# A gated layer's first product in block form: eleven block products for twelve, seven of them over two feature tiles

## The chip, the cores and the metric

The kernel runs on one core of a Trainium2 chip (trn2). The metric is the time of one execution on the device in microseconds (us). A core has a matrix engine (TensorE, PE in the profile, with its weight loads as PEld), VectorE (DVE), ScalarE (ACT) and GpSimd (POOL); SyncE (SP) issues most transfers. PE reads SBUF and writes PSUM, and each engine runs its own program in a fixed order, waiting on semaphores.

## The reference

Two stages. The first is a delta-rule recurrence over 768 steps for 4 x 8 heads of 48 features. The second is a gated two-layer network over its 3072 token rows.

```python
k_n = k / (np.linalg.norm(k, axis=-1, keepdims=True) + 1e-06)
for t in range(S):                       # S = 768, D = 48, batch 4, heads 8
    y[:, :, t] = np.einsum('bhd,bhde->bhe', q[:, :, t], state)
    v_old = np.einsum('bhde,bhd->bhe', state, kt)
    state = state + bt[:, :, :, None] * np.einsum('bhd,bhe->bhde', kt, vt - v_old)
x = y.transpose(0, 2, 1, 3).reshape(3072, 384)
h = x @ w_in                             # 384 x 2048
g = h * np.cos(h)
return g @ w_out                         # 2048 x 384
```

The inputs moe_w_in and moe_w_out arrive as 64-bit floats, which the kernel reads as pairs of 32-bit words and narrows on the chip.

## The kernel before

**Recurrence.** The steps are cut into 24 units of 32 steps (C), and two units make a pair: 12 pairs of 256 token rows (TOK). For each unit small matmuls form the Gram blocks (`gram`), pass the keys and queries through the state (`through_state`), solve (`solve`), update the state (`update`) and form the output (`within`). For each pair a triangular inverse is formed on POOL (`invert`, with the tiles `part` and `z`), between two trips through DRAM: g out and gb back, z out and zt back. `features` turns a unit's output into the layout that the network needs, the tile x_ffn (`xts[p]`): 128 features x 3 feature tiles (KT) x 256 rows.

**First gated layer** (`hidden`). The 2048 hidden features are 16 tiles of 128 (FT). For pairs 1 to 11 the layer takes two tiles at a time into one PSUM bank: for each, three matmuls of 128x128 weights over all 256 rows, accumulated over the feature tiles. Pair 0 alone takes four tiles for one unit, so 128 rows (`hidden_one`). Two banks (tag h) alternate. Each bank is then gated in four steps: `hidden_turns` (ACT, PSUM to whole turns), `hidden_rest` (DVE, the rest of the turn), `hidden_cos` (ACT, two instructions), `hidden_gate` (DVE, times h, into the tile g_ffn). The bank is held until the last step. All h are scaled by SCALE = 256, from the way the weights are narrowed.

**Second layer.** For pair 0 it is plain (`output`). For pairs 1 to 11 it is done in seven block products for eight (`product`), over units 1 and 2, even and odd hidden tiles, and two halves of the output columns: `left_sum` (DVE) forms sums of gated blocks in place, `right_sum` sums of the weights once, and `collect` adds the products up. `left(p, k, a)` picks a block from the gate tile.

**The order.** The program of every engine is written out by `Order`, a planner: each task has an engine, a cost, dependencies, buffers that it makes and uses, and a due time; it plays the tasks in simulated time and emits them in the order in which they start. `BASE`, `START`, `FIRST` and `STEP` set the due times of the gated work, `W_IN`, `W_OUT` and `LOADS` those of the weights, `bufs` the count of buffers of each tag. `STICK` lets PE stay among small or large matmuls a little longer, and `count` and `stall` model how PE's instructions are fetched in blocks of 256. `gated(p)` adds the tasks of a pair's first layer, `strassen(p)` those of its second.

**Buffers.** Gate tiles, weights on their way (`pairs`) and squares for the norms (`ksq`) share the tag g, with GATES = 9 slots of 128 x 1024. Keys wait in four tiles `kps`, each for a pair.

Of the kernel before, what the change touches and what calls it, by code (L numbers as in the profile page):

```python
# [46 lines left out]
class Order:  # L47
# [13 lines left out]
    STICK = 2.885  # L61
# [26 lines left out]
    def count(self, key):  # L88
        if key == ("state", 0):
            return 0  # L90
        return self.COUNT[key[0]] * (2 if key[:2] == ("hidden", 0) else 1)
# [139 lines left out]
def kernel(  # L231
# [45 lines left out]
    GATES = 9  # L277
# [35 lines left out]
    kps = [const.tile([128, 2, H, DP], FP, name=f"kp{i}") for i in range(4)]  # L313
# [87 lines left out]
    w_sum = const.tile([128, FT // 2, 3, HM], FP, name="w_sum")  # L401
    p_out = psum.tile([128, 2, 256], FP, name="p_out", tag="o", bufs=1)
# [196 lines left out]
    def invert(m, tag, columns):  # L599

        a, z = gbs[m], zs[m]
        eng = nc.gpsimd if tag is None else nc.vector
        for j in columns:
            rows = j // SPLIT + 1
            shape = [128, rows, C - 1 - j]
            if tag is None:
                part = work.tile([128, ROWS * C // 2], FP, name="part")  # L610
            else:
                part = ffn_pool.tile([128, ROWS * C // 2], FP, name="part_v", tag="o")
            part = part[:, 0 : shape[1] * shape[2]].rearrange(
                "p (r i) -> p r i", i=shape[2]
            )
            eng.tensor_tensor(  # L616
                out=part,
                in0=z[:, 0:rows, j, None].to_broadcast(shape),
                in1=a[:, j, None, j + 1 :].to_broadcast(shape),
                op=ALU.mult,  # L620
            )
            behind = z[:, 0:rows, j + 1 :]
            eng.tensor_tensor(out=behind, in0=behind, in1=part, op=ALU.subtract)  # L623
# [145 lines left out]
    def step_of(tile, p):  # L769
        return tile.rearrange("p a (b t) -> p (a b) t", t=128) if p == 0 else tile  # L770

    def hidden(p, f):
        if p == 0:
            return hidden_one(f)
        p_h = p_hs[p, f] = bank("h", [128, 2, TOK], "p_h")
        for i in range(2):
            for t in range(KT):
                nc.tensor.matmul(  # L778
                    p_h[:, i],
                    w_in[:, t, (f + i) * 128 : (f + i + 1) * 128],  # L780
                    xts[p][:, t],
                    start=(t == 0),
                    stop=(t == KT - 1),
                )


    TURN = 1.0 / (2.0 * math.pi * SCALE)

    def hidden_turns(p, f):
        turns[p, f] = step_of(ffn_pool.tile([128, 2, TOK], I32, name="turns"), p)  # L790
        nc.scalar.activation(turns[p, f], p_hs[p, f], AF.Copy, scale=TURN)  # L791

    def hidden_rest(p, f):
        r = rests[p, f] = step_of(ffn_pool.tile([128, 2, TOK], FP, name="r"), p)
        nc.vector.scalar_tensor_tensor(  # L795
            out=r, in0=p_hs[p, f], scalar=TURN, in1=turns.pop((p, f)),
            op0=ALU.mult, op1=ALU.subtract,
        )
# [6 lines left out]
    def hidden_gate(p, f):  # L805
        k = f // 2 % 4 if p == 0 else f // 4
        if (p, k) not in gates:
            gates[p, k] = ffn_pool.tile(
                [128, 4, TOK], FP, name="g_ffn", tag="g", bufs=GATES
            )  # L810
        if p == 0:
            out = gates[p, k][:, :, f // 8 * 128 : (f // 8 + 1) * 128]
        else:
            out = gates[p, k][:, f % 4 : f % 4 + 2]
        nc.vector.tensor_tensor(  # L815
            out=out,
            in0=rests.pop((p, f)),
            in1=p_hs.pop((p, f)),
            op=ALU.mult,
        )  # L820

# [25 lines left out]
    def left(p, k, a):  # L847

        unit, odd_tile = a // 10 - 1, a % 10 - 1
        return gates[p, k][:, odd_tile::2, unit * 128 : (unit + 1) * 128]  # L850
# [28 lines left out]
    def product(p, x, part):  # L879
        a, b = PRODUCTS[x]  # L880
        p_o = product_out(p, x)
        for e in range(4 * part, 4 * part + 4):
            nc.tensor.matmul(  # L883
                p_o,
                left(p, e // 2, a)[:, e % 2],
                right(e, b),
                start=(e == 0),
                stop=(e == FT // 2 - 1),
                skip_group_check=True,
            )  # L890

    def left_sum(p, x, k):
        to, one, two, op = {
            1: (21, 21, 22, ALU.add),
            2: (11, 21, 11, ALU.subtract),
            3: (22, 22, 11, ALU.subtract),
            4: (12, 12, 11, ALU.subtract),
        }[x]
        nc.vector.tensor_tensor(  # L899
            out=left(p, k, to), in0=left(p, k, one), in1=left(p, k, two), op=op  # L900
        )
# [40 lines left out]
    def store(p, i, cols=slice(0, DM)):  # L942
# [11 lines left out]
            x=2, turns=2, r=2, g=GATES, o=2, o_out=2,  # L954
# [5 lines left out]
    W_IN, W_OUT, LOADS = 68.978, 54.441, -24.919  # L960
    PLAIN = range(1)
    outs_done = [None]
    START = 60.385
    FIRST, STEP = 2.515, 5.309
# [127 lines left out]

    def gated(p):
        for f in range(0, FT, 2):
            deps = [("features_out", 2 * p + 1)]
            new = f % 4 == 0
            if p == 0:
                deps = [("features_out", f // 8)]
                deps += [("add", t) for t in range(KT * (f // 2 % 4 + 1))]
                new = f < 8  # L1100
            if p or f:
                deps.append(("hidden", p if f else p - 1, f - 2 if f else FT - 2))
            key = (p, f)
            add(("hidden", *key), "PE", 2.62, lambda f=f: hidden(p, f), deps,
                makes=[("h", ("h", *key))], uses=[("x", p)],
                due=BASE[p] + f // 2 * (STEP if p else FIRST))
            add(("turns", *key), "ACT", 0.65, lambda f=f: hidden_turns(p, f),
                [("hidden", *key)], makes=[("turns", ("turns", *key))])
            add(("rest", *key), "DVE", 0.73, lambda f=f: hidden_rest(p, f),
                [("turns", *key)], makes=[("r", ("r", *key))], uses=[("turns", *key)])  # L1110
            add(("cos", *key), "ACT", 1.45, lambda f=f: hidden_cos(p, f), [("rest", *key)])
            add(("gate", *key), "DVE", 0.73, lambda f=f: hidden_gate(p, f),
                [("cos", *key)] + ([] if new else [("gate", p, f - 2 if p else f - 8)]),
                makes=[("g", ("gates", p, f // 4 if p else f // 2))] if new else [],
                uses=[("h", *key), ("r", *key)], due=BASE[p] + f // 2 * STEP + 8)
        if p in PLAIN:
            plain(p)
        else:
            strassen(p)
# [27 lines left out]
    def strassen(p):  # L1147
# [4 lines left out]
        for step, x in enumerate(products(p)):  # L1152
            tag = "h" if p == LAST and (p + step) % 2 else "o"
            for part in range(2):
                ks = (2 * part, 2 * part + 1)
                deps = [last] if last else []
                if x in (1, 2, 4):
                    deps += [("gate", p, 4 * k + f) for k in ks for f in (0, 2)]
                else:
                    deps += [("left", p, {6: 2, 5: 1, 3: 4, 7: 3}[x], k) for k in ks]  # L1160
                for e in (4 * part, 4 * part + 2):
                    if x in (1, 2, 3):
                        deps += [("add", 12 + t) for t in range(2 * e + 4)]
                    deps.append(("right", {6: 2, 4: 4, 5: 1, 7: 3}.get(x, 1), e))
                last = ("out", p, step, part)
                add(last, "PE", 1.31, lambda x=x, part=part: product(p, x, part), deps,
                    makes=[] if part else [(tag, ("p_o", p, x))],
                    uses=[("gates", p, k) for k in ks],
                    due=due(step + 0.5 * part))
                for k in ks:  # L1170
                    if x == 1:
                        add(("left", p, 1, k), "DVE", 0.46, lambda k=k: left_sum(p, 1, k),
                            [("gate", p, 4 * k), ("gate", p, 4 * k + 2)])
                        add(("left", p, 2, k), "DVE", 0.46, lambda k=k: left_sum(p, 2, k),
                            [("left", p, 1, k), last])
                    elif x in (2, 4):
                        sx = {2: 4, 4: 3}[x]
                        add(("left", p, sx, k), "DVE", 0.46,
                            lambda k=k, sx=sx: left_sum(p, sx, k), [("left", p, 2, k), last])
# [28 lines left out]

    def weights(t):
# [16 lines left out]
    for p in sorted(PLAIN):  # L1226
        gated(p)
    weight_sums()
    for p in range(len(PLAIN), NU // 2):
        gated(p)  # L1230
# [63 lines left out]
```

## Time and profile before

| what | before |
|---|---|
| runs shown, us | 699.57, 694.07, 699.24; median 699.24 |
| profiled execution, us | 697.96 |
| its span, us, and mean granted PE clock | 696.1, 0.99 |
| PE busy | 627.9 us, 90% |
| PE weight loads busy | 554.6 us, 80% |
| DVE busy | 418.1 us, 60% |
| ACT busy | 266.3 us, 38% |
| POOL busy | 341.4 us, 49% |
| bytes moved | 52.41 MB, mean 75 GB/s |

The page of the profile shows one execution. Its lines with forty digits cut the span in slices of 17.4 us, each digit the busy share in tenths. A group's line gives source line, engine, operation, tile written <- tiles read, shapes and count, then after the bar the busy time and the mean length of one instruction in ns, and after the second bar the engine's idle time before them with what ended it. A matmul of float32 appears as two instructions, each with its own weight load. Instructions of PE are pipelined, so that a matmul's length is more than its spacing to the next one.

### The profile page before, as it was taken

The page shows a single profiled execution, that of the slowest core. Times are in us where ns is not written, and L with a number is a line of the kernel's source. Part 1 is how long each engine was busy: PE and PEld are TensorE (multiplying, and loading weights), DVE is VectorE, ACT ScalarE, POOL GpSimd, SP SyncE. Part 2 cuts the span into 40 slices and gives each one's busy share as a digit, 9 for nine tenths or more (in the row PEclk, how much of TensorE's full clock was granted, in tenths as well). Part 3 has the DMA queues.
Part 4 walks back from the last instruction along what each step waited for, and adds up shares of the span by engine and source line. Part 5 has one row for each costly group of instructions (what it writes and reads, how often), then busy time and mean ns, then how long its engine had stood idle before and what let it go on. Part 6 is the DMA issues. An engine that isn't in the chain of part 4 may idle for free.

```text
span 696.1 us, 25073 instructions
## 1 busy us (share of the span) xinstructions
PE 627.9 (90%) x10968; PEld 554.6 (80%) x10968; DVE 418.1 (60%) x820; ACT 266.3 (38%) x450; POOL 341.4 (49%) x734
## 2 busy tenths in 40 slices
PE   4213699899999999999999999999989999999997
PEld 3103588676888898888898988888878988988996
DVE  5696578985674665565565565565556455444542
ACT  3433367662442342433433342432422342433430
POOL 5458768967803825816806806807618308300000
PEclk9999999999999999999999999999999999999999
DMA  8797575643434325235245245253122120100000
GB/s 171 175 205 169 117 217 135 126 78 69 70 44 84 55 48 97 51 60 96 45 67 93 41 62 96 40 90 64 26 61 48 32 48 26 30 12 16 1 24 23
DMA packets 213969, 52.41 MB, mean 75 GB/s; under 512 B 205412, under 2 KB 208628, under 8 KB 213860
## 3 DMA queue, kind: packets, MB, share of 16 engines
q1 hardware_dynamic: 211428, 49.97, 36.6%
q8 instruction: 86, 1.41, 0.8%
q10 hardware_dynamic: 2176, 0.39, 0.3%
q0 software_dynamic: 256, 0.44, 0.3%
q14 instruction: 23, 0.19, 0.1%
HBM read 39.76 MB, written 11.01 MB: 73 GB/s over the span
## 4 chain that ended last, share of the span: by engine, by line
PE 76%; DMA 10%; DVE 5%; SPq 3%; ACT 2%; POOL 2%; issue 2%; ACTq 0%; POOLq 0%; DVEq 0%
PE p_h L778 31%; PE p_out L883 28%; PE p_kq L658 4%; DMA pairs<-in_moe_w_in_dram 3%; SPq L341 3%; PE p_kq L723 3%; PE p_s L706 2%; PE p_u L685 2%; PE p_g L547 2%; PE p_out L825 2%; DMA gb<-g_dr 2%; PE p_o L883 1%; DMA out_dram<-o 1%; DMA kp<-in_k_dram 1%; DVE pairs L437 1%
## 5 line engine op out<-in xcount | busy, mean ns | idle before, releaser
L778 PE MATMUL p_h<-x_ffn,w_in 128*128 128x256 f32 x1056 | 243.5, 384 | 3.6 <-DVE g_ffn L815 3.4
L616 POOL TENSOR_TENSOR part<-z,gb 128x126 f32<-128x126 f32 (+22 forms) x341 | 132.3, 388 | 206.4 <-DMA gb<-g_dr 109.9
L778 PEld LDWEIGHTS p_h<-x_ffn,w_in 128*128 128x128 f32 x1056 | 198.2, 191 | 32.8 <-issue 5.1
L623 POOL TENSOR_TENSOR z<-z,part 128x126 f32<-128x126 f32 (+22 forms) x341 | 137.4, 403 | 26.7
L883 PE MATMUL p_out<-w_out,g_ffn 128*128 128x192 f32 x672 | 125.8, 333 | 0.9
L791 ACT ACTIVATE turns<-p_h 128x512 int32<-128x512 f32 x96 | 57.0, 593 | 158.8 <-PE p_h L778 156.3
L795 DVE SCALAR_TENSOR_TENSOR r<-p_h,turns 128x512 f32<-128x512 f32 x96 | 65.9, 686 | 83.9 <-ACT turns L791 83.8
L883 PEld LDWEIGHTS p_out<-w_out,g_ffn 128*128 128x128 f32 x672 | 108.8, 190 | 6.6 <-ACT o L920 3.3
L802 ACT ACTIVATE r<-r 128x512 f32<-128x512 f32 x96 | 60.4, 629 | 92.1 <-DVE r L795 92.0
L883 PE MATMUL p_out<-w_sum,g_ffn 128*128 128x192 f32 x496 | 90.0, 331 | 1.1 <-issue 0.7
L899 DVE TENSOR_TENSOR g_ffn<-g_ffn 128x256 f32<-128x256 f32 x176 | 79.4, 470 | 17.6 <-PE p_out L883 16.1
L815 DVE TENSOR_TENSOR g_ffn<-r,p_h 128x512 f32<-128x512 f32 x96 | 65.3, 680 | 37.7 <-ACT r L803 37.7
L883 PEld LDWEIGHTS p_out<-w_sum,g_ffn 128*128 128x128 f32 x496 | 83.2, 192 | 3.5 <-issue 1.0
L803 ACT ACTIVATE r<-r,halfpi 128x512 f32<-128x512 f32 x96 | 69.3, 722 | 3.1
L933 DVE SCALAR_TENSOR_TENSOR o<-p_out,o 128x192 f32<-128x192 f32 x74 | 25.3, 354 | 48.8 <-PE p_out L883 48.5
L475 POOL TENSOR_TENSOR knrm<-ksum,halves 128x16 f32<-128x16 f32 (+1 forms) x14 | 36.7, 2618 | 12.9 <-DVE ksum L463 12.2
L658 PE MATMUL p_kq<-st,kq_t 48*32 48x48 f32 x2944 | 33.1, 217 | 2.6 <-issue 2.0
L658 PEld LDWEIGHTS p_kq<-st,kq_t 48*32 48x32 f32 x2944 | 29.7, 107 | 6.7 <-issue 5.8
L437 DVE SCALAR_TENSOR_TENSOR pairs<-pairs 128x384 uint32<-128x384 uint32 (+1 forms) x28 | 23.4, 835 | 12.7 <-ACT pairs L433 12.6
L734 ACT COPY y<-p_kq 128x384 f32<-128x384 f32 x24 | 11.5, 478 | 48.3 <-PE p_kq L723 48.2
L516 PE MATMUL p_t<-consts,kp 128*128 128x128 f32 x32 | 7.7, 390 | 21.5 <-DVE p_i L623 11.3
L714 DVE TENSOR_TENSOR st<-st,p_s 128x768 f32<-128x768 f32 x22 | 20.9, 949 | 9.5 <-PE p_s L706 9.5
(74 smaller groups left out, 584.0 us busy)
## 6 DMA issues: line engine op xcount, KB each, us to landing
pairs<-in_moe_w_in_dram SPq DMA_DIRECT2D x12, 512.0 KB
gb<-g_dr SPq DMA_DIRECT2D x24, 256.0 KB
pairs<-in_moe_w_out_dram SPq DMA_DIRECT2D x16, 384.0 KB
kp<-in_k_dram SPq DMA_DIRECT2D x96, 48.0 KB
vp<-in_v_dram SPq DMA_DIRECT2D x96, 48.0 KB
out_dram<-o SPq DMA_DIRECT2D x23, 192.0 KB
g_dr<-g SPq DMA_DIRECT2D x24, 128.0 KB
z_dr<-z SPq DMA_DIRECT2D x12, 256.0 KB
```

The source lines that it names most:

```text
L475: nc.gpsimd.tensor_tensor(out=scales[m][2][:, part], in0=sums[m, part.start][:, 0:n], in1=halves[:, 0:n], op=ALU.pow,)
L616: eng.tensor_tensor(out=part, in0=z[:, 0:rows, j, None].to_broadcast(shape), in1=a[:, j, None, j + 1 :].to_broadcast(shape), op=ALU.mult,)
L623: eng.tensor_tensor(out=behind, in0=behind, in1=part, op=ALU.subtract)
L658: nc.tensor.matmul(p_kq[quarter(b), par, a, j], kq_t[rows48(par), a, b * NP + j], st[rows48(par), b // 2, j, b % 2], start=(j == 0 and a = ...
L778: nc.tensor.matmul(p_h[:, i], w_in[:, t, (f + i) * 128 : (f + i + 1) * 128], xts[p][:, t], start=(t == 0), stop=(t == KT - 1),)
L791: nc.scalar.activation(turns[p, f], p_hs[p, f], AF.Copy, scale=TURN)
L795: nc.vector.scalar_tensor_tensor(out=r, in0=p_hs[p, f], scalar=TURN, in1=turns.pop((p, f)), op0=ALU.mult, op1=ALU.subtract,)
L802: nc.scalar.activation(r, r, AF.Abs)
L803: nc.scalar.activation(r, r, AF.Sin, bias=halfpi, scale=-2.0 * math.pi)
L815: nc.vector.tensor_tensor(out=out, in0=rests.pop((p, f)), in1=p_hs.pop((p, f)), op=ALU.mult,)
L883: nc.tensor.matmul(p_o, left(p, e // 2, a)[:, e % 2], right(e, b), start=(e == 0), stop=(e == FT // 2 - 1), skip_group_check=True,)
L899: nc.vector.tensor_tensor(out=left(p, k, to), in0=left(p, k, one), in1=left(p, k, two), op=op)
```

## The change

The first layer of pairs 1 to 11 is no longer 3 feature tiles x all rows, but block products. A block is four hidden tiles, even or odd (`odd_tile`), of one half (`s`) of the sixteen, by one unit's 128 rows. For feature tiles 0 and 1 the four blocks of (even, odd) x (unit 0, unit 1) come from seven products of sums for eight products; feature tile 2 adds four plain products. That is eleven for twelve, run as eight layer steps (`STEPS`), of which steps 1, 6 and 7 hold two products.

- New sums: `x_sum` (DVE, once a pair, partly in place in x_ffn), and `in_sums` (DVE, once in the run, into `in_sum` and partly in place in w_in, after pair 0 has used w_in).
- Each PSUM bank (`BANK`) is emptied by `layer_out`: ACT copies it, or DVE adds it to an earlier block, into the gate tile. Steps 0, 2, 4 and 6 go on accumulating in one bank, with a copy after each.
- The gating then works on the gate tile in SBUF in place, not on PSUM; `hidden_rest` writes over the turns, and the tile r is gone.
- A gate tile is now one unit x (even, odd) x four hidden tiles, so that `left` is one contiguous block of 512 and `left_sum` runs once a half rather than twice.
- For room in SBUF: GATES 8 for 9, three `kps` for four, one `part` for two, no r.
- Planner: `gated` splits into `gated_plain` (pair 0, as before) and the new `gated`; STICK, START, FIRST, STEP, W_IN, W_OUT and LOADS have new values.

```diff
-    STICK = 2.885
+    STICK = 3.659
...
+        if key[0] == "layer":
+            return 32 if key[3] in (1, 6, 7) else 16
...
-    GATES = 9
+    GATES = 8
...
-    kps = [const.tile([128, 2, H, DP], FP, name=f"kp{i}") for i in range(4)]
+    kps = [const.tile([128, 2, H, DP], FP, name=f"kp{i}") for i in range(3)]
...
+    in_sum = const.tile([128, 3, FT // 2, 128], FP, name="in_sum")
...
-                part = work.tile([128, ROWS * C // 2], FP, name="part")
+                part = work.tile([128, ROWS * C // 2], FP, name="part", bufs=1)
...
+    def hidden_of(p, f):
+        return p_hs[p, f] if p == 0 else place(p, f)
+
     def hidden_turns(p, f):
-        turns[p, f] = step_of(ffn_pool.tile([128, 2, TOK], I32, name="turns"), p)
-        nc.scalar.activation(turns[p, f], p_hs[p, f], AF.Copy, scale=TURN)
+        turns[p, f] = ffn_pool.tile([128, 4, 128], I32, name="turns")
+        nc.scalar.activation(turns[p, f], hidden_of(p, f), AF.Copy, scale=TURN)
 
     def hidden_rest(p, f):
-        r = rests[p, f] = step_of(ffn_pool.tile([128, 2, TOK], FP, name="r"), p)
+        t = turns.pop((p, f))
+        r = rests[p, f] = t.bitcast(FP)
         nc.vector.scalar_tensor_tensor(
-            out=r, in0=p_hs[p, f], scalar=TURN, in1=turns.pop((p, f)),
+            out=r, in0=hidden_of(p, f), scalar=TURN, in1=t,
             op0=ALU.mult, op1=ALU.subtract,
         )
...
     def hidden_gate(p, f):
...
+        nc.vector.tensor_tensor(
+            out=place(p, f), in0=rests.pop((p, f)), in1=hidden_of(p, f), op=ALU.mult
+        )
...
+    def x_sum(p):
+        xt = xts[p]
+        t = x_sums[p] = ffn_pool.tile([128, 3, 128], FP, name="x_sum", bufs=1)
+        u0, u1 = slice(0, 128), slice(128, 256)
+        for to, one, two in (
+            (t[:, 1], xt[:, 1, u1], xt[:, 0, u1]),
+            (xt[:, 0, u1], xt[:, 0, u1], xt[:, 0, u0]),
+            (t[:, 0], xt[:, 1, u1], xt[:, 0, u1]),
+            (t[:, 2], xt[:, 1, u0], t[:, 0]),
+        ):
+            nc.vector.tensor_tensor(out=to, in0=one, in1=two, op=ALU.subtract)
...
+    def in_sums(s, x):
+        es = slice(4 * s, 4 * s + 4)
+        even0, odd0 = in_block(0, 0, es), in_block(0, 1, es)
+        to, one, two, op = {
+            3: (in_sum[:, 1, es], even0, odd0, ALU.subtract),
+            1: (odd0, odd0, in_block(1, 1, es), ALU.add),
+            2: (in_sum[:, 0, es], odd0, even0, ALU.subtract),
+            4: (in_sum[:, 2, es], in_block(1, 0, es), in_sum[:, 0, es], ALU.subtract),
+        }[x]
+        nc.vector.tensor_tensor(out=to, in0=one, in1=two, op=op)
+
+    STEPS = {
+        0: [(0, 0, 0, 0)],
+        1: [(1, 0, 1, 0), (2, 0, 2, 0)],
+        2: [("s", 0, "t", 0)],
+        3: [("s", 1, "t", 1)],
+        4: [(0, 1, 0, 1)],
+        5: [(2, 1, 2, 1)],
+        6: [("s", 2, 1, 1), (2, 0, 2, 1)],
+        7: [(1, 1, "t", 2), (2, 1, 2, 0)],
+    }
+    BANK = {0: 0, 2: 0, 4: 0, 6: 0, 1: 1, 3: 3, 5: 3, 7: 7}
+
+    def layer(p, s, i):
+        first = BANK[i] == i
+        if first:
+            p_hs[p, s, i] = bank("h", [128, 4, 128], "p_h")
+        p_h = p_hs[p, s, BANK[i]]
+        for a, odd_tile, b, unit in STEPS[i]:
+            for e in range(4):
+                f = 2 * (4 * s + e) + odd_tile
+                nc.tensor.matmul(
+                    p_h[:, e],
+                    in_sum[:, odd_tile, 4 * s + e]
+                    if a == "s" else w_in[:, a, f * 128 : (f + 1) * 128],
+                    x_sums[p][:, unit]
+                    if b == "t" else xts[p][:, b, unit * 128 : (unit + 1) * 128],
+                    start=first and e == 0,
+                    stop=True,
+                    skip_group_check=True,
+                )
+            first = False
...
+    def layer_out(p, s, i):
+        p_h = p_hs[p, s, BANK[i]]
+        if i % 2 == 0:
+            to = {0: (0, 0), 2: (1, 0), 4: (1, 1), 6: (1, 0)}[i]
+            nc.scalar.copy(block(p, s, to), p_h)
+        else:
+            to, one = {
+                1: ((0, 0), (0, 0)), 3: ((0, 1), (1, 0)), 5: ((1, 1), (1, 1)),
+                7: ((0, 1), (0, 1)),
+            }[i]
+            nc.vector.tensor_tensor(
+                out=block(p, s, to), in0=block(p, s, one), in1=p_h, op=ALU.add
             )
...
-    W_IN, W_OUT, LOADS = 68.978, 54.441, -24.919
+    W_IN, W_OUT, LOADS = 44.42, 59.45, -41.818
...
-    START = 60.385
-    FIRST, STEP = 2.515, 5.309
+    START = 65.512
+    FIRST, STEP = 2.57, 5.606
...
+        last = ("layer", p - 1, 1, 7) if p > 1 else ("hidden", p - 1, FT - 2)
+        weights = {0: (), 1: (), 2: (2,), 3: (3,), 4: (1,), 5: (), 6: (4,), 7: ()}
...
+            for i in range(8):
+                count = len(STEPS[i])
+                deps = [last, ("features_out", 2 * p + 1)]
+                deps += [("in_sums", x, s) for x in weights[i]]
+                if i in (2, 3, 4, 7):
+                    deps.append(("x_sum", p))
+                deps += {2: [out(0)], 4: [out(2)], 5: [out(3)], 6: [out(4)]}.get(i, [])
+                last = key = ("layer", p, s, i)
+                at = BASE[p] + (4 * s + i / 2) * STEP
+                add(key, "PE", 0.875 * count, lambda s=s, i=i: layer(p, s, i), deps,
...
+            for i, f in ((1, (0, 0)), (5, (1, 1)), (6, (1, 0)), (7, (0, 1))):
+                gating(p, (s, *f), [out(i)], [], [], BASE[p] + (4 * s + i / 2) * STEP + 8)
```

## The prediction

> **What bounds the kernel now.** I read the engines' busy shares and the forty slices first, to see which engine is full and when.
>
> ```profile
> PE 627.9 (90%) x10968; PEld 554.6 (80%) x10968; DVE 418.1 (60%) x820; ACT 266.3 (38%) x450; POOL 341.4 (49%) x734
> PE   4213699899999999999999999999989999999997
> DVE  5696578985674665565565565565556455444542
> ```
>
> One slice is 17.4 us. TensorE (PE) is full from slice 5 (87 us) to the end; VectorE (DVE) is near full only in slices 6 to 8 (104 to 157 us). Next come stretches of 50 us, about one pair of units each. The columns are length, then busy time (and count) of PE, PE's weight loads, DVE, ACT, POOL.
>
> ```profile
> 125.00:175.00 50.00, 47.65 (x655) 35.23 (x658) 38.59 (x68) 23.94 (x42) 38.22 (x71) 0.97 0.51 94
> 325.00:375.00 50.00, 49.91 (x918) 44.63 (x917) 29.84 (x59) 18.68 (x31) 25.42 (x59) 1.00 0.39 68
> 625.00:675.00 50.00, 49.91 (x510) 46.01 (x509) 23.23 (x48) 19.07 (x31) 0.00 (x0) 1.00 0.04 13
> ```
>
> In the steady part PE has 0.09 us free in 50, while DVE has 20 and ACT 31. So less PE work is less time, one for one, as long as PE finds its inputs ready. The chain that ended last says what PE does there, and the groups say in what pieces.
>
> ```profile
> PE p_h L778 31%; PE p_out L883 28%; PE p_kq L658 4%; DMA pairs<-in_moe_w_in_dram 3%; SPq L341 3%; PE p_kq L723 3%; PE p_s L706 2%; PE p_u L685 2%; PE p_g L547 2%; PE p_out L825 2%; DMA gb<-g_dr 2%; PE p_o L883 1%; DMA out_dram<-o 1%; DMA kp<-in_k_dram 1%; DVE pairs L437 1%
> L778 PE MATMUL p_h<-x_ffn,w_in 128*128 128x256 f32 x1056 | 243.5, 384 | 3.6 <-DVE g_ffn L815 3.4
> L761 PE MATMUL p_h<-x_ffn,w_in 128*128 128x128 f32 x192 | 24.2, 280 | 1.3 <-issue 0.9 <-POOL w_in L446 0.4
> ```
>
> The first gated layer of pairs 1 to 11 (L778) is the largest entry: 1056 instructions, that is 11 pairs x 48 matmuls, each as two instructions. It waited only 3.6 us. L761 is pair 0's first layer, the only place where the trace shows the 128-column form that the change uses everywhere. A mean of a matmul is its latency, not its spacing; the spacing is read from runs on PE's timeline (start, length):
>
> ```profile
> 383.57 5.34 PE L778 MATMUL p_h<-x_ffn,w_in 128*128 128x256 f32 x24
> 101.85 2.84 PE L761 MATMUL p_h<-x_ffn,w_in 128*128 128x128 f32 x24
> 106.25 2.94 PE L761 MATMUL p_h<-x_ffn,w_in 128*128 128x128 f32 x24
> ```
>
> Taking off the last one's latency (medians 379 and 275 ns): (5.34 - 0.379)/23 = 215.7 ns for 256 columns; (2.84 - 0.275)/23 = 111.5 ns for 128, or 115.9 ns in the second run. Half of 215.7 would be 107.9. The narrow form costs 3% or more over half.
>
> [...] The trace's median for L899 (256) is 424, so I use 691 for the 512 forms. [...] L899's mean is 470 against its median of 424, so I add 46 ns to each such instruction.
>
> **The change part by part.** Times are made against the profiled execution's 697.96 us (span 696.1 and 1.9 around it).
>
> *PE's first layer, pairs 1 to 11.* Before: 96 x 215.7 ns = 20.71 us a pair. After: eleven block products x 2 halves of the feature tiles x 4 tiles = 88 matmuls of 128 columns, 176 instructions x 111.5 = 19.62 us. Saved 1.09 a pair, 12.0 over 11 pairs. Ends: at 107.9 ns, 19.0 saved (the whole twelfth); at 115.9, 3.4. I take 12.0, because 111.5 comes from the undisturbed run.
>
> *DVE per pair.* Out: eight rests and eight gates from PSUM (8 x 686 + 8 x 680 = 10.9 us) and sixteen left sums (79.4/11 = 7.2). In: rests, gates and eight wider left sums, 24 x (691+46) = 17.7; eight layer_out adds from PSUM, shaped as L815, 8 x 680 = 5.4; x_sum, four sums of 128, 4 x (291+46) = 1.3. Sum 24.4 for 18.1: +6.3, so DVE goes from 30 to 36 us of about 49, 74%. Its free 20 us hide this on average.
>
> *ACT per pair.* Eight PSUM copies of 512 as in kq_t<-p_t (583 ns): +4.7, to 23 of 49 us. Hidden by 31 free us.
>
> *The new waits on PE.* Each layer i from 2 to 6 waits for the layer_out two steps back, or for that step's bank. A step is 0.89 us (8 x 111.5) or twice that; ACT's copy with its hand-overs is about 0.6 + 0.3, so back to back a layer would wait about 0 to 0.2 us, more if DVE's queue holds it. Behind a waiting layer on PE stand the second layer's products and the small matmuls of the recurrence, all in fixed order. The planner can place a product half (1.30 us) or small work between two layers: two layers fall due per 5.6 us, and PE has some 29 us of other work a pair. Bounds: 0, and 0.12 us at each of 176 pieces[...], 21 us. Below nothing: a bank is now released by one copy or add instead of the four-step gating, and L778's idle of 3.6 us may go. I take 0.2 a pair, +2.
>
> *The start.* Eight in_sums (512 elements, both in SBUF, 0.74 each: 5.9 us), the first x_sum (1.3) and pair 1's extra 5 us fall on DVE at 117 to 175 us, where it is busy 38.6 of 50. That gives about 51 us in 50. Pair 0's plain outputs (L825, 64 instructions x 323 ns = 20.7 us) can fill PE, and the surplus spills into the next stretch, which has 19 us of DVE free. Bounds: -3 (a PE gap of 2.35 us at 136.5, waiting for g_ffn, goes) to +12 (all of the addition shows). I take +3.5.
>
> *The end.* After the last layer PE needs gates that pass two more instructions each; three gatings lie close together there (layers 5, 6 and 7), about 2 us of ACT each. Held-back products cover it now: after the last L778 at 670 us PE runs on unbroken. The first product needs only the first-gated tile, so its two halves and half the next are cover too: 3.9 us. I take +0.5, bounds 0 and 3.
>
> *Buffers and queues.* Three kp tiles for four: a load (383.7 us) to its pair's last update (480) spans 96 us, under three periods of 50.5; SP's k loads now wait for an update three pairs back, and nothing queues behind them late. Eight gate slots for nine: two pairs hold four each, and the squares for the norms (1.9 us a pair) fit only while a pair's products have given tiles back. Without that cover the norms come later and with them POOL's inverse; POOL idles some 24 us a pair. One `part` buffer: POOL's multiply already needs the subtract before it. POOL meets more and longer two-input DVE instructions, about 18 per inverse for 10; at an estimated 0.1 us each (two of L899's 46 ns) that is +1 to 2 us in 29. It is hidden while zt still lands before its solve: in one pair the zt transfers were issued from 349.9 to 354.8 us and the solve began at 359.9, a margin of about 3 to 5 us; past that PE waits for it. PE issues 160 more instructions a pair (a load and a matmul each), 1760 in all or 7 more blocks of 256[...]. Its stalls belong to the small matmuls (1.99 us of issue at 510 us); their positions shift, +-3. All these: 0.
>
> *Sum.* -12.0 + 2 + 3.5 + 0.5 = -6.0: 692.0 on the profiled execution. The median of the runs shown lies 1.3 above it (699.24 to 697.96), so 693.3.
>
> **Rivals.**
>
> *A. The saving arrives whole.* PE's fill takes the new waits and the start costs nothing: -12 or a little more, 686 to 688, so 687. For it: 20 free us on DVE, and banks free sooner. Against: DVE's full stretch at the start.
>
> *B. PE stalls at the layer steps, slower.* One mechanism: layer_out stands in DVE's or ACT's in-order queue behind gating work, the next layer comes late, and all of PE with it. The place is every pair from 175 to 640 us. It decides once the mean lateness passes 12.0 us/176 = 68 ns a piece. At 0.12 us, 21 us are lost: -12 + 21 + 3.5 = +12.5, so 711.8. For it: DVE at 74% with 0.7 us instructions, so an average arrival finds one running. Against: products and small work can be put between, and no wait of this size stands on PE before.
>
> *C. The narrow form isn't cheaper in total.* If broken runs of 8 or 16 hold 117.7 ns, 176 x 117.7 = 20.71 and nothing is saved: -0 + 6 = 705.2. The second L761 run (115.9) speaks for it, the first against.
>
> **How the numbers follow.** The sum (693.3, own range 687 to 700) has 0.55, A 0.15, B 0.17, C 0.13. About 1%, 7 us, is what a measurement of this kernel can tell from no change. The sum's case gives 0.21 to faster and 0.34 to same; A is faster; B is slower; C falls 0.11 slower and 0.02 same. So faster 0.36, same 0.36, slower 0.28. The range 684 to 711 leaves out about half of B above and a few hundredths of A below.
>
> **What would show it.** Right: matmul runs of the new layer at 110 to 113 ns; PE's first-layer share of a pair near 19.6 us; periods of about 49.6 for 50.5; DVE near 36 us in 50 with PE at 49 or more; some us of new PE idle at 120 to 180 us. Wrong: PE idle before the layer matmuls, released by layer_out, over 1 us a pair (B); spacings of 116 or more (C); POOL's inverse over 33 us and PE waiting for zt.

## The result, and the profile after

The changed kernel takes 739.15 us (median of 4, 738.01 to 740.66) against 698.96 for the kernel before on the same chip: ratio 1.0593, 95% interval 1.054 to 1.0645. It is slower, by about 40 us. Lines of the changed kernel differ by a few: 616/623 (GpSimd's inverse) became 620/627, 685 (solve) 689, 883 (product) 962, 933 (collect) 1012; 874 is the new layer, 893 and 899 its copies and adds, 836 x_sum, 978 the left sums.

Busy shares and slices of the changed kernel, then its core's span and mean granted clock:

```profile
PE 635.5 (86%) x11848; PEld 592.3 (80%) x11848; DVE 491.4 (67%) x871; ACT 315.9 (43%) x538; POOL 404.0 (55%) x734
PE   4107698989999989899799979989799979999997
PEclk9999799999999999999899999999899998999999
...
core 0: 738.6 us, clock 0.966
```

PE no longer stays at 9 after slice 5. POOL's busy time is 404.0 for 341.4, though its 734 instructions are the same. The whole from 125 to 675 us, for the kernel before and then for the changed one, and two stretches of the changed one (columns as before; the first number after POOL's is the mean granted clock):

```profile
125.00:675.00 550.00, 541.87 (x9051) 478.42 (x9051) 323.15 (x604) 208.48 (x344) 257.92 (x601) 0.99 0.31 56
...
125.00:675.00 550.00, 508.15 (x9690) 475.81 (x9689) 363.97 (x606) 234.28 (x391) 323.63 (x614) 0.97 0.32 57
...
325.00:375.00 50.00, 44.91 (x708) 42.42 (x708) 29.85 (x50) 21.72 (x36) 29.10 (x63) 0.93 0.34 60
625.00:675.00 50.00, 49.87 (x912) 47.77 (x899) 31.35 (x53) 23.48 (x39) 25.84 (x50) 1.00 0.11 21
```

PE is idle for 550 - 508.15 = 41.9 us there, for 550 - 541.87 = 8.1 before. From 625 us, when the last inverse runs (618.8 to 654.7 us) and no other comes after it, PE is full again. The chain that ended last, and the groups that matter:

```profile
PE 35%; POOL 34%; DMA 15%; issue 6%; SPq 4%; DVE 4%; ACT 2%; POOLq 0%; ACTq 0%; DVEq 0%
POOL z L627 16%; POOL part L620 16%; PE p_h L874 13%; PE p_out L962 13%; DMA gb<-g_dr 5%; DMA g_dr<-g 2%; DMA z_dr<-z 2%; PE p_u L689 2%; SPq L343 2%; PE p_h L765 2%; PE p_kq L662 1%; DMA qp<-in_q_dram 1%; SPq L645 1%; DMA pairs<-in_moe_w_in_dram 1%; PE p_o L962 1%
...
L620 POOL TENSOR_TENSOR part<-z,gb 128x126 f32<-128x126 f32 (+22 forms) x341 | 163.1, 478 | 196.7 <-DMA gb<-g_dr 147.3
L627 POOL TENSOR_TENSOR z<-z,part 128x126 f32<-128x126 f32 (+22 forms) x341 | 167.4, 491 | 26.7
...
L899 DVE TENSOR_TENSOR g_ffn<-g_ffn,p_h 128x512 f32<-128x512 f32 x88 | 60.1, 683 | 45.0 <-PE p_h L874 43.8
L805 DVE SCALAR_TENSOR_TENSOR turns<-g_ffn,turns 128x512 f32<-128x512 f32 x88 | 65.1, 740 | 27.9 <-ACT turns L800 27.9
L978 DVE TENSOR_TENSOR g_ffn<-g_ffn 128x512 f32<-128x512 f32 x88 | 65.3, 746 | 8.2 <-PE p_out L962 8.0
```

POOL's inverse, no part of the listed chain before, is now 32% of it. Its 682 instructions went from 132.3 + 137.4 = 269.7 us (388 and 403 ns each) to 330.5 (478 and 491). On POOL's timeline an inverse, from its first `part` to the end of its last `z`, takes 34.9 us (mean of pairs 3 to 11) for 28.7 before. DVE's new instructions cost what was reckoned: 740 and 746 ns where 737 stood, 683 where 680 stood. The 691 ns in that 737 and the 291 of x_sum were the author's estimates; the runs bear them out. On DVE in the kernel before, forms with both inputs in SBUF take 291 ns for 128 columns (L616) and a median of 424 for 256 (L899), a line that reaches 690 at 512; in the changed kernel the medians are 692 (L805, L816) and 693 (L978), and the shortest x_sum takes 291. So DVE's own times are not what went wrong.

Why POOL is slower shows on the timelines of DVE and POOL side by side (start, length):

```profile
406.93 0.68 DVE L978 TENSOR_TENSOR g_ffn<-g_ffn 128x512 f32<-128x512 f32 x1
406.94 0.92 POOL L627 TENSOR_TENSOR z<-z,part 128x96 f32<-128x96 f32 x1
...
520.55 0.39 POOL L627 TENSOR_TENSOR z<-z,part 128x96 f32<-128x96 f32 x1
```

The same POOL form takes 0.39 us at 520.55, with no DVE instruction beside it, and 0.92 when it starts 10 ns after a DVE instruction with two SBUF inputs: it loses 0.53 us, most of DVE's 0.68.

This holds over the whole run. Take each POOL instruction of the inverse against the median of its form with no DVE instruction beside it, a median that is the same in both kernels within about 10 ns (forms that never ran alone are left out), and put the excess down to the DVE instruction that it overlaps most. In the changed kernel 178 of the 264 instructions of L805, L816 and L978 (512 columns, both inputs in SBUF) overlap an inverse and cost it 63 us, 0.35 us each. The adds of L899 are as wide, but with one input in PSUM: 58 overlap, and cost it 0.1 us in all. In the kernel before, 88 left sums (256 columns, both in SBUF) cost 0.09 us each.

How this reaches PE shows around 439 us, merged from four engines:

```profile
434.50 0.23 POOL L627 TENSOR_TENSOR z<-z,part 128x16 f32<-128x16 f32 x1
434.69 2.90 POOL L479 TENSOR_TENSOR knrm<-ksum,halves 128x16 f32<-128x16 f32 x1
437.62 0.17 DVE L490 TENSOR_SCALAR knrm<-knrm 128x16 f32<-128x16 f32 x1 [5.42 <-POOL knrm L479]
438.64 0.35 DVE L1012 SCALAR_TENSOR_TENSOR o<-p_out,o 128x192 f32<-128x192 f32 x1
439.05 1.27 PE L962 MATMUL p_out<-w_out,g_ffn 128*128 128x192 f32 x3 [4.08 <-DVE o L1012]
```

The late inverse holds back the norms' root (knrm, 2.90 us) behind it on POOL. DVE's scaling stands at the head of its queue for 5.42 us (2.8 at the most in the kernel before), with a collect behind it, and PE waits 4.08 us for that collect. No semaphore says "POOL" at PE; the wait carries another engine's name. Among PE's waits from 125 to 675 us (sum, count and longest in us) are:

```profile
PE p_h L874 <- ACT g_ffn L893: 9.1, 6, 3.5
...
PE p_g L551 <- DVE tt L571: 7.0, 4, 2.6
...
PE p_u L689 <- DMA zt<-z_dr: 5.7, 7, 3.5
...
PE p_h L874 <- DVE x_sum L836: 4.2, 1, 4.2
PE p_out L962 <- DVE o L1012: 4.1, 1, 4.1
```

Most of the longer gaps cost twice. After seven of the eight gaps of over 2 us from 125 us on, the granted clock is halved for 3.4 or 6.8 us (after the eighth, 2.60 us at 492.5, it is not; one such stretch, at 217.3, follows gaps of 0.8 us at the most). One of them, with the granted clock of the stretch after it (0.50, the third number from the end):

```profile
358.79 2.08 PE L874 MATMUL p_h<-x_ffn,w_in 128*128 128x128 f32 x8 [3.55 <-ACT g_ffn L893]
360.66 2.77 PE L962 MATMUL p_out<-w_sum,g_ffn 128*128 128x192 f32 x8
...
365.40 1.06 PE L874 MATMUL p_h<-x_ffn,w_in 128*128 128x128 f32 x8
366.30 1.47 PE L962 MATMUL p_out<-w_sum,g_ffn 128*128 128x192 f32 x8
...
358.79:364.04 5.25, 5.25 (x20) 5.25 (x21) 2.80 (x5) 1.94 (x3) 4.54 (x10) 0.50 0.01 2
```

Eight layer matmuls take 2.08 us and then 1.06. Over the run, (1 - 0.966) x 738.6 = 25.1 us of full clock are missing for (1 - 0.990) x 696.1 = 7.0 before. So, as an estimate, +33.8 (idle) + 18.1 (clock) - 12.0 (the layer's saving, as reckoned and shown below) = +39.9, of a span longer by 42.5. The terms aren't quite apart: the idle is from 125 to 675 us and the clock over the whole span, and three of the half-clock stretches begin up to 1.6 us before their gap ends. The remaining 2.6 isn't placed.

### The profile page after: what moved, and what is told of

Same layout as the page of the kernel before. It is cut to its first block, busy times and chain, and to the rows that moved or that the text cites. A ratio compares the mean times of both kernels' runs of the same rounds, so it can differ in the third digit from the quotient of the medians.

```text
span 738.6 us, 27047 instructions
## 1 busy us (share of the span) xinstructions
PE 635.5 (86%) x11848; PEld 592.3 (80%) x11848; DVE 491.4 (67%) x871; ACT 315.9 (43%) x538; POOL 404.0 (55%) x734
## 4 chain that ended last, share of the span: by engine, by line
PE 35%; POOL 34%; DMA 15%; issue 6%; SPq 4%; DVE 4%; ACT 2%; POOLq 0%; ACTq 0%; DVEq 0%
POOL z L627 16%; POOL part L620 16%; PE p_h L874 13%; PE p_out L962 13%; DMA gb<-g_dr 5%; DMA g_dr<-g 2%; DMA z_dr<-z 2%; PE p_u L689 2%; SPq L343 2%; PE p_h L765 2%; PE p_kq L662 1%; DMA qp<-in_q_dram 1%; SPq L645 1%; DMA pairs<-in_moe_w_in_dram 1%; PE p_o L962 1%
## 5 line engine op out<-in xcount | busy, mean ns | idle before, releaser
L874 PE MATMUL p_h<-x_ffn,w_in 128*128 128x128 f32 x1232 | 161.8, 281 | 7.2 <-ACT g_ffn L893 4.3
L874 PEld LDWEIGHTS p_h<-x_ffn,w_in 128*128 128x128 f32 x1232 | 153.7, 197 | 9.7 <-ACT g_ffn L893 4.7
L800 ACT ACTIVATE turns<-g_ffn 128x512 int32<-128x512 f32 x88 | 55.3, 629 | 119.4 <-DVE g_ffn L899 115.6
L893 ACT COPY g_ffn<-p_h 128x512 f32<-128x512 f32 x88 | 51.1, 580 | 94.6 <-PE p_h L874 94.4
L899 DVE TENSOR_TENSOR g_ffn<-g_ffn,p_h 128x512 f32<-128x512 f32 x88 | 60.1, 683 | 45.0 <-PE p_h L874 43.8
L805 DVE SCALAR_TENSOR_TENSOR turns<-g_ffn,turns 128x512 f32<-128x512 f32 x88 | 65.1, 740 | 27.9 <-ACT turns L800 27.9
L812 ACT ACTIVATE turns<-turns 128x512 f32<-128x512 f32 x96 | 60.2, 627 | 48.9 <-DVE turns L805 48.3
L816 DVE TENSOR_TENSOR g_ffn<-turns,g_ffn 128x512 f32<-128x512 f32 x88 | 64.2, 730 | 11.9 <-ACT turns L813 11.4
L978 DVE TENSOR_TENSOR g_ffn<-g_ffn 128x512 f32<-128x512 f32 x88 | 65.3, 746 | 8.2 <-PE p_out L962 8.0
L813 ACT ACTIVATE turns<-turns,halfpi 128x512 f32<-128x512 f32 x96 | 69.3, 722 | 3.1
L874 PE MATMUL p_h<-x_sum,in_sum 128*128 128x128 f32 x352 | 50.2, 288 | 9.9 <-ACT g_ffn L893 4.8
L1012 DVE SCALAR_TENSOR_TENSOR o<-p_out,o 128x192 f32<-128x192 f32 x74 | 25.3, 354 | 30.5 <-PE p_out L962 29.3
L662 PE MATMUL p_kq<-st,kq_t 48*32 48x48 f32 x2944 | 33.8, 212 | 3.2 <-issue 1.9
```

The costliest lines, as they stand in the source:

```text
L800: nc.scalar.activation(turns[p, f], hidden_of(p, f), AF.Copy, scale=TURN)
L805: nc.vector.scalar_tensor_tensor(out=r, in0=hidden_of(p, f), scalar=TURN, in1=t, op0=ALU.mult, op1=ALU.subtract,)
L812: nc.scalar.activation(r, r, AF.Abs)
L813: nc.scalar.activation(r, r, AF.Sin, bias=halfpi, scale=-2.0 * math.pi)
L816: nc.vector.tensor_tensor(out=place(p, f), in0=rests.pop((p, f)), in1=hidden_of(p, f), op=ALU.mult)
L874: nc.tensor.matmul(p_h[:, e], in_sum[:, odd_tile, 4 * s + e] if a == "s" else w_in[:, a, f * 128 : (f + 1) * 128], x_sums[p][:, unit] if b ...
```

## The experiments

Theory 1: the inverse, slowed by DVE's two-SBUF instructions, runs late against an order that was written for some 30 us of it, and the other engines wait behind it in their fixed queues. Theory 2: the short layer steps wait for their own copies and adds. "Idle" is PE's, from 125 to 675 us; "inverse" is the mean of pairs 3 to 11. Each ratio is to the kernel before in the same comparison. Idle, inverse and clock are of the one profiled run: for b_due this is its fastest (700.03 us).

| run | us | ratio, 95% interval | idle | inverse | clock |
|---|---|---|---|---|---|
| before (profiled run) | 697.96 | 1 | 8.1 | 28.7 | 0.990 |
| after | 739.15 | 1.059 [1.054, 1.065] | 41.9 | 34.9 | 0.966 |
| a_trim | 709.06 | 1.013 [0.9995, 1.027] | 23.6 | 28.8 | 0.982 |
| b_stretch | 740.05 | 1.058 [1.043, 1.072] | 36.8 | 35.2 | 0.973 |
| b_sbuf | 710.17 | 1.015 [0.999, 1.031] | 13.9 | 32.4 | 0.983 |
| a_plan | 716.00 | 1.023 [1.011, 1.035] | 30.5 | 34.2 | 0.981 |
| b_cut | 689.87 | 0.987 [0.983, 0.990] | 7.9 | 6.1 | 0.996 |
| a_cut | 697.54 | 0.9995 [0.997, 1.002] | 20.2 | 7.6 | 0.995 |
| a_tuned1 | 685.34 | 0.982 [0.979, 0.986] | 10.1 | 34.2 | 0.999 |
| a_tuned2 | 686.96 | 0.984 [0.980, 0.988] | 12.0 | 34.1 | 0.989 |
| a_ksq | 738.70 | 1.055 [1.049, 1.061] | 42.4 | 35.1 | 0.966 |
| a_trim_ksq | 705.16 | 1.006 [1.003, 1.010] | 20.2 | 29.4 | 0.984 |
| b_due | 704.73 | 1.009 [1.006, 1.012] | 12.2 | 28.8 | 0.997 |

**a_trim: the changed kernel with a shorter inverse.**

```diff
         for j in columns:
+            if tag is None and j > 24:
+                continue
             rows = j // SPLIT + 1
```

> The changed kernel, with GpSimd's inverse shortened: its last six columns (25 to 30) are left out in pairs 1 to 11, everything else in the same order. That takes about 5 us off each inverse (35 us in the changed kernel), to some 30 us, what the planner counts. Theory 1 (the inverse, slowed by VectorE's instructions with two SBUF inputs, runs late against a fixed order, and PE, SP, ACT and DVE wait behind it): PE's idle time after 125 us falls from 42 us to under 15, and the run takes 695 to 710 us. Theory 2 (the short layer steps wait for their own layer_out): nothing changes for them, 733 to 740 us.

Measured: 709.06 us, idle 23.6. The inverse is 28.8 us again, and 30 of the 40 us are gone with no instruction of PE, DVE or ACT changed or moved. Theory 2 expected nothing. But the idle time was to fall under 15 us and is 23.6, still 15 over the kernel before: not all of the loss is the inverse's.

**b_stretch: the kernel before with a longer inverse.**

```diff
                 op=ALU.mult,
             )
+            if tag is None and 8 <= j < 20:
+                eng.tensor_tensor(
+                    out=part,
+                    in0=z[:, 0:rows, j, None].to_broadcast(shape),
+                    in1=a[:, j, None, j + 1 :].to_broadcast(shape),
+                    op=ALU.mult,
+                )
```

> The kernel before, with twelve multiplies of each GpSimd inverse (columns 8 to 19, pairs 1 to 11) issued twice, so that an inverse takes about 35 us for 28.6; order and results are the same. Theory 1: the same lateness as in the changed kernel, without its layer, costs 25 to 50 us: 725 to 750 us. Theory 2: GpSimd is off the path, under 5 us: 698 to 704 us.

Measured: 740.05 us. The inverse takes 35.2 us, and the kernel with its old first layer becomes as slow as the changed one. Its chain reads alike:

```profile
POOL 42%; PE 30%; DMA 10%; issue 8%; SPq 4%; DVE 4%; ACT 1%; POOLq 0%; ACTq 0%
```

Six us more of POOL in a pair are enough for the whole loss, though POOL is busy for 54% of that span.

**b_sbuf: the kernel before with the gating's inputs in SBUF.**

```diff
+    stand_in = w_in[:, 0, 0 : 2 * TOK].rearrange("p (a t) -> p a t", a=2)
...
-            out=r, in0=p_hs[p, f], scalar=TURN, in1=turns.pop((p, f)),
+            out=r, in0=p_hs[p, f] if p == 0 else stand_in, scalar=TURN, in1=turns.pop((p, f)),
...
-            in1=p_hs.pop((p, f)),
+            in1=p_hs.pop((p, f)) if p == 0 else stand_in,
```

> The kernel before in its own order, but for pairs 1 to 11 the DVE instructions hidden_rest and hidden_gate take a block of w_in in SBUF in place of the PSUM bank, so that both inputs lie in SBUF as in the changed kernel; the values that are gated are stand-ins. Nothing is added to any engine, and the banks come free earlier. If two SBUF inputs are what slows GpSimd: the inverse goes from 28.6 to 31 to 34 us, DVE's instructions from 0.69 to 0.74, and the run takes 705 to 730 us. If GpSimd was slowed by something else in the change: inverse at 28 to 29 us and the run at 690 to 700 us.

Measured: 710.17 us; the ratio's interval reaches 1, so the time alone doesn't show that the run got longer. The inverse's mean is 32.4 us for 28.7. Its groups:

```profile
L616 POOL TENSOR_TENSOR part<-z,gb 128x126 f32<-128x126 f32 (+22 forms) x341 | 147.6, 433 | 190.9 <-DMA gb<-g_dr 148.8
L623 POOL TENSOR_TENSOR z<-z,part 128x126 f32<-128x126 f32 (+22 forms) x341 | 157.1, 461 | 26.7
...
L796 DVE SCALAR_TENSOR_TENSOR r<-w_in,turns 128x512 f32<-128x512 f32 x88 | 67.2, 764 | 77.3 <-ACT turns L792 77.3
L816 DVE TENSOR_TENSOR g_ffn<-r,w_in 128x512 f32<-128x512 f32 x88 | 63.6, 723 | 33.6 <-ACT r L804 33.3
```

POOL's inverses take 304.7 us for 269.7: +35.0 for 176 DVE instructions, 0.20 us each, though only 92 of them overlap an inverse (0.37 us each, counted as above). No instruction was added to POOL or DVE; the place of one input is the only edit. So the slowing of POOL is shown, without the block products.

**a_plan: the changed kernel, the planner told the inverse's true cost.**

```diff
-            each = (0.2, 0.001) if held else (0.323, 0.00178)
+            each = (0.2, 0.001) if held else (0.378, 0.00208)
```

> The changed kernel, with the planner told of a dearer GpSimd inverse (0.378 us + 0.00208 us per element for 0.323 and 0.00178, a factor 1.17 as measured: 35 us for 29.9), so that the order leaves room for it; no instruction is added or left out. Theory 1: PE's idle time after 125 us falls from 42 us to under 20, 700 to 720 us. Theory 2: 730 to 745 us. A new order also shifts other waits, which may cost or bring 5 to 10 us.

Measured: 716.00 us with an inverse nearly as long as without this edit, 34.2 us. The idle time, 30.5 us, misses the 20 that was expected. Nearly half of it is one hole in the start that the new order has:

```profile
143.74 1.56 PE L710 MATMUL p_s<-u,kp 64*64 64x96 f32 x32 [14.09 <-DVE tt L571]
```

From the first to the last matmul of the layer (153.7 to 689.0 us) it needs 535.3 us, where the kernel before needed 545.2 (124.7 to 669.9) and the changed one 591.5 (121.5 to 713.0). In that stretch the slow inverse costs little once the order knows of it.

**b_cut and a_cut: both kernels with most of the inverse left out.**

```diff
         for j in columns:
+            if tag is None and j > 7:
+                continue
```

> The kernel before without most of GpSimd's inverse: columns 8 to 30 are left out in pairs 1 to 11, some 8 us are left of 28.6, all else in the same order. It is the base for the next kernel. PE bounds the kernel before, so both theories expect little: 690 to 700 us, PE idle after 125 us at 3 to 8 us.

> The changed kernel with the same columns left out, so with GpSimd out of the way. It shows what the first layer in block form is worth by itself. Theory 1 (the inverse's lateness is all that went wrong): 12 us of PE work less, some of it lost at the start, so 5 to 14 us under the kernel before cut in the same way, about 682 to 692 us. Theory 2 (layer steps wait for layer_out): at or above it, 700 us or more, with PE idle over 20 us in front of the layer's matmuls.

Measured: 689.87 (just under its range) and 697.54 us. Here theory 1 fails as it was put: with POOL out of the way the changed kernel should lie under the other, and it lies 7.7 us above it, with 20.2 us of idle for 7.9. Its order has late places that are not the inverse's. PE's waits in a_cut name nearly all of them: 7.7 us for ACT's copies, in six places; 9.6 as "issue", time in which PE waited for nothing that the profile shows (3.2 in the kernel before); 1.3 for x_sum. For two of the six copies the way can be read. One of them:

```profile
280.69 0.84 ACT L462 ACTIVATE ksq<-kp 128x768 f32<-128x768 f32 x1 [4.95 <-DMA vp<-in_v_dram]
281.44 0.57 ACT L895 COPY g_ffn<-p_h 128x512 f32<-128x512 f32 x1
282.06 1.16 PE L876 MATMUL p_h<-x_sum,in_sum 128*128 128x128 f32 x8 [2.50 <-ACT g_ffn L895]
```

The squares for the norms (ksq) stand at the head of ACT's queue for 4.95 us until a load lands, the copy stands behind them, and PE waits 2.50 us for the copy; at 339.30 us it is 2.33 us in the same way.

**a_ksq and a_trim_ksq: the squares without their wait.** A candidate for the rest: in the changed kernel `ACT ksq` waits up to 7.1 us for a key load at the head of ACT's queue, and layer_out's copies stand behind it.

```diff
-        nc.scalar.square(ksq[:, 0:n], kps[m % len(kps)][:, part, :, 0:D])
+        src = kps[m % len(kps)][:, part, :, 0:D]
+        if m >= 4:
+            src = w_in[:, 2, 0 : n * H * D].rearrange("p (u h d) -> p u h d", u=n, h=H)
+        nc.scalar.square(ksq[:, 0:n], src)
```

> The changed kernel, but from pair 4 on ACT's squares for the norms (ksq) read a part of w_in that is long in place, in place of the key tile, so that this instruction no longer waits for a load at the head of ACT's queue, with layer_out's copies behind it; the norms of those pairs are stand-ins. The loads themselves stay as late as they are. If ACT's queue is the way by which late loads reach PE: the gaps of 2 to 4 us before the layer's matmuls go, and the run takes 720 to 730 us for 739. If the late inverse itself holds PE (zt, and POOL's other work): 735 to 740 us.

> Both edits on the changed kernel: the inverse without its last six columns, and the squares without their wait for a load. If these two are the whole of the loss against this order, PE's idle after 125 us falls from 24 us (with the first alone) to under 12 and the run takes 690 to 702 us for 709; if the layer's steps still wait for their copies, 705 to 710 us.

Measured: 738.70 and 705.16 us. Alone the edit does nothing: the waits for ACT's copies went and PE waits for other results as long (42.4 us idle). With the shorter inverse the time is 4 us lower, which two runs of a_trim (707.09 and 711.03) hardly tell from nothing, and 20.2 us of idle stay where under 12 were expected: PE's waits for ACT's copies fell from 7.4 to 0.4 us, and those for DVE's tt and o rose from 0.9 to 5.6. ACT's queue was a way of the loss; as the whole of what the inverse leaves it falls.

**a_tuned1 and a_tuned2: the changed kernel with true costs and other due times.**

```diff
-    STICK = 3.659
+    STICK = 5.134
...
-    W_IN, W_OUT, LOADS = 44.42, 59.45, -41.818
+    W_IN, W_OUT, LOADS = 48.473, 62.498, -23.134
...
-    START = 65.512
-    FIRST, STEP = 2.57, 5.606
+    START = 83.292
+    FIRST, STEP = 3.130, 5.676
...
-            each = (0.2, 0.001) if held else (0.323, 0.00178)
+            each = (0.2, 0.001) if held else (0.39, 0.00215)
...
-        add(("x_sum", p), "DVE", 1.1, lambda: x_sum(p), [("features_out", 2 * p + 1)],
+        add(("x_sum", p), "DVE", 1.6, lambda: x_sum(p), [("features_out", 2 * p + 1)],
```

(In both, WINDOW changes too, here from 129.466 to 129.427. a_tuned2: STICK 5.432, W_IN, W_OUT, LOADS 48.396, 56.786, -33.381, START 86.971, FIRST, STEP 3.223, 5.479, WINDOW 161.374; costs as here.)

> The changed kernel with the planner's inverse at 0.39 us + 0.00215 us per element and x_sum at 1.6 us, and with new due times (START, FIRST, STEP, W_IN, W_OUT, LOADS, STICK), chosen so that the order at the start has no hole before pair 1's first layer. Same instructions. Theory 1: no waits for zt, PE's idle after 125 us under 12 us, 684 to 698 us, so 2 to 15 us under the kernel before. Theory 2: 715 us or more.

> As the one before it, with another set of due times and a wider WINDOW (161). It shows how much hangs on the one choice: theory 1 again 684 to 698 us, within 8 us of the other set; theory 2 715 us or more.

Measured: 685.34 and 686.96 us, ratios 0.982 [0.979, 0.986] and 0.984 [0.980, 0.988]. Both are faster than both kernels, by less than 2% against the kernel before but with intervals well clear of 1, and with the changed kernel's instructions. Of a_tuned1: the whole from 125 us, one stretch, a POOL group, and the waits of PE for the new layer:

```profile
125.00:675.00 550.00, 539.88 (x10198) 510.08 (x10191) 395.26 (x665) 251.98 (x428) 313.93 (x610) 1.00 0.32 56
...
325.00:375.00 50.00, 50.00 (x1005) 47.75 (x1005) 39.15 (x64) 22.75 (x39) 35.56 (x67) 1.00 0.39 67
...
L620 POOL TENSOR_TENSOR part<-z,gb 128x126 f32<-128x126 f32 (+22 forms) x341 | 158.2, 464 | 143.3 <-DMA gb<-g_dr 102.5
...
PE p_h L874 <- DVE g_ffn L899: 3.4, 3, 1.6
...
PE p_h L874 <- ACT g_ffn L893: 1.0, 2, 0.5
```

POOL is nearly as slow as in the changed kernel (an inverse takes 34.2 us for 34.9), PE is full, its waits for zt are 0.2 us for 5.7, and in 176 layer pieces PE waits 4.4 us for copies and adds: 25 ns a piece. All of its idle time, 10.1 us, would be 57 ns a piece. So theory 2 is not a price of the new layer itself: in the order that came with the change PE waits 10.7 us for copies and adds (9.1 and 1.6), in an order that fits 4.4. The layer runs from 126.9 to 658.6 us, 531.7 for 545.2.

**b_due: the kernel before with a_tuned1's due times and inverse cost.**

> The kernel before, with the planner's inverse cost and the due times of the faster version of the changed kernel (a_tuned1), to see whether those alone bring its 12 us. If the block products bring them: 695 to 720 us, no faster than the kernel before. If the due times do: about 685 us.

Measured: 704.73 us, 1.009 [1.006, 1.012]. These due times bring the old layer nothing, so in a_tuned1 the 12 us come with the block products. Due times chosen anew for the kernel before were not run; what they would bring is not known.

## Why the prediction was wrong

- **The step that failed** is the line on buffers and queues: "POOL meets more and longer two-input DVE instructions, about 18 per inverse for 10; at an estimated 0.1 us each (two of L899's 46 ns) that is +1 to 2 us in 29. It is hidden while zt still lands before its solve". Size: the inverse grew by 6.2 us, 28.7 to 34.9. The price was taken from DVE's side, from how much L899 is stretched on average. The side that loses most is POOL: 0.35 us for each wide DVE instruction that overlaps an inverse, 0.53 in the pair of lines shown. The count was about right: 178 in eleven inverses, 16 each. That POOL's inverse passes 33 us and PE waits for zt is the last of the signs of being wrong that the prediction lists, and it came.
- POOL's side could have been priced from the trace of before, where once a pair L504, a wide DVE instruction with both inputs in SBUF, falls on an inverse (start, length):

```profile
386.55 0.98 DVE L504 TENSOR_TENSOR vp<-vp,knrm 128x768 f32<-128x768 f32 x1 [2.15 <-DMA kp<-in_k_dram]
386.80 1.03 POOL L623 TENSOR_TENSOR z<-z,part 128x130 f32<-128x130 f32 x1
```

  The POOL form takes 0.44 us (median) with no DVE instruction beside it. Counted as above, eleven such overlaps cost 6.8 us, 0.62 each. Taken per column, 512 columns would have been some 0.4 us and 18 instructions some 7 us an inverse, an estimate from these numbers; the overlaps of the three new groups come to 63 us in eleven inverses, 5.7 each, for 0.7 each of the left sums in the kernel before.
- **"Hidden" was wrong too.** The margin of 3 to 5 us was named, and 6.2 passes it. The prediction named zt as the first to be late. That came (PE's waits for it: 5.7 us), but more went through queues: POOL to DVE's scale to a collect; POOL to SP's put of z, for which SP waits 203.9 us in all for 109.4, with loads behind it. Only moved lateness was priced, not what stands behind the late instruction on each engine. Nor did "nothing queues behind them late", said of SP's key loads, hold: in a_cut, without the long inverse, the squares wait up to 4.95 us at the head of ACT's queue for a load (2.1 in the kernel before), and copies and PE wait behind them. Whether the three kp tiles are why was not run.
- **The clock** had no term: 18.1 us by the two means, so that by the estimate above idle of 33.8 us cost about half as much again.
- **PE's first layer: right.** The layer's matmuls are spaced as reckoned:

```profile
518.08 2.84 PE L874 MATMUL p_h<-x_ffn,w_in 128*128 128x128 f32 x24
```

  (2.84 - 0.275)/23 = 111.5 ns, so 12.0 us saved; a_tuned1's layer is 13.5 us shorter in all, and its run 11.8 under the kernel before. The rival without a saving (C) falls.
- **New waits, +2:** in the changed kernel they can't be told from the inverse's. In a_cut, with the inverse short, PE waits 7.7 us for copies; in a_tuned1 4.4 for copies and adds. The 0.3 us for a copy's hand-overs was an estimate that came out too high: in the changed kernel a copy starts 37 ns after the matmul it waited for (L893, median of 59), and a layer matmul 53 ns after the copy it waited for (six). Rival B's 0.12 us a piece was the author's estimate, with no measurement under it. Rival B, the slower one, named the wrong main mechanism: a late copy at each of 176 pieces would have left a_trim and a_tuned1 as slow. What it described happens in a few places only.
- **The start, +3.5, and the end, +0.5:** neither came. The layer begins at 121.5 us for 124.7, and from its last matmul to the last product it is 20.3 us (713.0 to 733.3) for 20.9.
- **The sum** had the change in an order that fits it in mind, and even there its -6.0 is too little: a_tuned1 lies 11.8 us under the kernel before in the same comparison, close to rival A's whole saving of 12.
- **Still open:** a_cut lies 12 us above a_tuned1 although its inverse is short. Its waits are read above: copies behind the squares, and 9.6 us of "issue" for 2.0 in a_tuned1. Why "issue" costs that much in this order was not settled. The instruction queue (q8 on the page) carries 93 packets in the changed kernel for 86, which fits blocks of 256 of PE's instructions with their loads (23696 for 21936); how much of "issue" belongs to them was not shown. x_sum is no part of it: its four instructions take 0.40 to 0.44 us each in the changed kernel, where the planner counts 1.1 for the four, but in a_cut, mostly clear of the inverse, their median is 0.29.

## What to carry to other kernels

In a program whose order is written out ahead, an instruction's price has to be reckoned for the engine that it slows, not only for the one that runs it, and the planner's costs for that other engine have to be measured anew: here a GpSimd stretch 6 us longer in each 50 us cost 39 us in the old kernel (b_stretch) and 30 of 40 in the changed one (a_trim), with GpSimd busy about half of the time. Moving DVE's inputs from PSUM to SBUF is such a change (b_sbuf: +35.0 us on GpSimd for 176 instructions). When a planned order meets a price that it doesn't know, the late instruction holds whatever stands behind it in each queue: here PE waited 4.08 us for a collect that stood behind DVE's late scaling. When a large change loses, shorten the suspect with all else in its place, and lengthen it in the old kernel; if both move the time alike, the change itself may still be worth its reckoned gain in a corrected order.

## What the runs showed of the hardware that was not expected

- A DVE instruction of 512 columns with both inputs in SBUF cost GpSimd's inverse 0.35 us where the two overlapped (178 in the changed kernel), one of 256 columns 0.09 us (88 in the kernel before), and one of 512 with an input in PSUM next to nothing (58, 0.1 us in all). In b_sbuf the place of one input alone made the difference: +35.0 us for 176 instructions. DVE's own instruction grew too, by about 50 ns on average (L805: median 692, mean 740): its mean was 766 ns for the 59 that overlapped a GpSimd instruction and 687 for the 29 that did not.
- In the changed kernel seven of eight PE gaps of 2.2 to 4.2 us were followed by spells in which PE ran at half its clock: 2.08 us for eight matmuls that take 1.06. The total of idle time doesn't fix the loss: the mean granted clock was 0.966 with 41.9 us of idle and 0.999 with 10.1 (a_tuned1), but 0.984 with 20.2 (a_trim_ksq) and 0.995 with 20.2 (a_cut).
- The narrow matmul form kept 111.5 ns at full clock in the new layer, for 107.9 at half of the wide form.
